# One-tile middle visits for a weight fold on two alternating PSUM banks, and one operand of the output stage made ahead of four copies

## The chip, the cores and the metric

The kernel runs on one core of a Trainium2 chip. The metric is the device time of one execution in microseconds (us), as the median of several runs. All times of single instructions come from one profiled execution of the same kernel. Engines are named as in the profile: PE is TensorE (PEld its weight loads), DVE is VectorE, ACT is ScalarE, POOL is GpSimd, and SP is SyncE, which here only issues DMAs.

## The reference, cut to what matters

Two blocks share one input `x` of 2048 tokens by 1024 features, and a gate mixes them. Block A is softmax attention with 32 heads of 32 dimensions. Block B picks, for each token and each of 32 heads, one of 64 experts by two small score tables, and adds a gated product of that expert's rows of `u` and `v`.

```
qkv = x @ wqkv                                # [2048, 3*1024], 32 heads of 32
p   = softmax(q @ k^T * 32**-0.5)             # per head
a   = (p @ v) @ wo
q1, q2 = split(x @ w_q)                       # 32 heads, 128 + 128 values each
s1, s2 = q1 @ k1^T, q2 @ k2^T                 # 8 scores each
i1, i2 = argmax(s1), argmax(s2)               # expert i1*8 + i2, one per head
b   = sum over heads of gelu(x . u[expert]) * v[expert]
g   = sigmoid(sum(x * gate_w))
out = g * a + (1 - g) * b
```

The kernel never forms `x @ w_q`. Since only the scores are wanted, it multiplies `w_q` with the differences of the rows of `k1` and `k2` first. This product of two weights is the "fold", and the change is about how it is laid into the program.

## The kernel before

Everything is float32. Most products run as three passes over a high and a low part (`split`, line 93: ACT writes the high part, DVE subtracts it). Large matrix products use a scheme with seven block products, `P1` to `P7`, in place of eight; a block product is 12 matmuls of 128x512 (`product`, lines 296 to 304, and `Halves.product`, whose matmuls are on line 964).

**Projection of q and k (0 to 377 us).** Two halves of the tokens times eight column chunks of the weight make 16 units. Units 0 and 8 are plain; `unit(u)` (line 483) makes the others, in the order P1, P5, P6, P2, P7, P3, P4, with the weight chunk of unit u+2 (`wraw`, 1 MB) loaded on SP's queue before P2. ACT and DVE prepare the next unit's operands between the products, and POOL issues the stores of q and k. Products rotate over PSUM banks 0 to 5.

**The fold inside it.** `w_q` comes as 32 tiles (`wqt`), each 1 MB in two halves of 512 KB, in four half-sized buffers, so two tiles at a time (line 313). A tile is four matmuls of 32x512 (line 341). Four tiles are a group; they accumulate in one bank, ACT copies the bank out (line 346), and later `fold_t` (line 351) transposes it in four matmuls on PE, ACT copies that (line 361), and POOL stores it. `fold()` (line 330) is a visit: it takes two tiles and then issues the loads of the next two (`load_wqs`, line 317). There is a visit after P4 of most units (`FOLDS`, line 478, and two more outside `unit`), and in the units of `MID_FOLDS` = {4, 11, 13} (line 479) a second one between P2 and P7 (line 540). All groups accumulate in bank 6, and all transposes go to bank 7. The order of each engine is the order in which the code is written, since the schedule is manual.

**Router, values, attention (377 to 1655 us).** These stages are not touched.

**Output (from 1655 us).** Eight blocks of 256 tokens are multiplied by `wo`. Blocks 0 and 1 are plain sums in banks 0 to 3 (`pa`) and 4 to 7 (`pa1`); `plain_out` (line 1582) copies the four banks to four places of one tile `post` (named `rb` in the profile), ACT and DVE in turns, and SP stores each. Both blocks use the same four places, so block 1's copies wait until block 0's stores have read them. Blocks 2 to 7 are made by `unit(n)` (line 1663) in the order P1, P7, P5, P6, P2, P3, P4, with short matmuls with `vhl` (line 1530) ahead of P2 to P4. Each product takes the next of eight banks: P1 bank 0, P7 bank 1, P5 bank 2, P6 bank 3, P2 bank 4, P3 bank 5, and so on, the same in every block. The operands `A11`, `S3`, `S1`, `S2`, `A12`, `S4`, `A22` come from the attention output (`scale_o`, line 1573, then `ht.operand`: DVE forms a sum on line 946 if the name begins with S, ACT makes the high part on line 94, DVE the low part on line 95). P7 needs S3, P5 needs S1, P6 needs S2. For block 2 only, the first four operands are made before `unit`, and S2, S4, A22 after P1's copy and after `plain_out(1, pa1)` (lines 1680 to 1683). In each block the sums that read P6, P7 and P5 out of PSUM (lines 1693 to 1696, recorded under the helper's line 970) are written behind the next block's A11, S3 and S1, so DVE does them in that order.

Of the kernel before, what the change touches and what calls it, by code (L numbers as in the profile page):

```python
# [9 lines left out]
F32 = mybir.dt.float32  # L10
F32R = mybir.dt.float32r
I32 = mybir.dt.int32
AF = mybir.ActivationFunctionType
# [6 lines left out]
KC = D // 128  # L20
HC = KC // 2
# [10 lines left out]
def gated_mha_peer_kernel(ctx, tc, xT, wqkv, wv, wo, wq, k12, ug, v, out):  # L32
# [8 lines left out]
    nc = tc.nc  # L41
# [72 lines left out]
    def bank_at(i):  # L114
        return ps1.tile([128, 512], F32, name=f"bk{i}")
# [3 lines left out]
    ev = Pool("ev", bufs=3)  # L119
    x8 = Pool("x8")  # L120
# [190 lines left out]
    def load_wq(n):  # L311
        for half in range(2):
            t = wqp.tile([128, 2, 512], F32, name="wqt", bufs=4)
            dma(t, wq[n // 4, n % 4][:, half * 1024:(half + 1) * 1024].rearrange("p (a m) -> p a m", a=2))
            wq_t[n, half] = t

    def load_wqs():
        n = fold_no[0]
        for m in range(n, min(n + 2, 32)):
            load_wq(m)  # L320

    def kpad_diffs():
        nc.gpsimd.memset(kpad, 0.0)
# [1 line left out]
            nc.gpsimd.tensor_tensor(out=kpad[:, :, i, 7 * i:7 * i + 7], in0=kraw[:, :, 1:],  # L325
                                    in1=kraw[:, :, 0:1].to_broadcast([128, 2, 7]), op=OP.subtract)

    fold_ps, fold_no, pending = [], [0], []

    def fold(load=True):  # L330

        for _ in range(2):
            n = fold_no[0]
            fold_no[0] += 1
            i = n % 4
            if i == 0:
                fold_ps[:] = [bank_at(6)]
            ps, = fold_ps
            t = wq_t.pop((n, 0)), wq_t.pop((n, 1))
            for quad in range(4):  # L340
                nc.tensor.matmul(ps[32 * quad:32 * quad + 32, :], kpad[:, quad % 2, i, :],  # L341
                                 t[quad // 2][:, quad % 2, :], start=(i == 0), stop=(i == 3))
        if i == 3:
            wt = (ev.tile([128, 512], F32, name="u4", bufs=1) if n // 4 == 3 else
                  x8.tile([128, HC, 512], F32, name="x8")[:, 0])
            nc.scalar.activation(wt, ps, AF.Copy)
            pending.append((n // 4, wt))
        if load:
            load_wqs()

    def fold_t():
        if not pending:
            return
        gi, wt = pending.pop(0)
        b, dh = divmod(gi, 2)
        pt = bank_at(7)
        for dc in range(4):
            nc.tensor.transpose(pt[:, dc * 128:(dc + 1) * 128], wt[:, dc * 128:(dc + 1) * 128], ident)
        wt2 = ev.tile([128, 512], F32, name="u7", bufs=1)[:, :448].rearrange(
            "p (a q r) -> p a q r", a=4, q=4)  # L360
        nc.scalar.activation(wt2, pt.rearrange("p (a q r) -> p a q r", a=4, q=4)[:, :, :, :28], AF.Copy)
        dma(WPD[:, 4 * dh:4 * dh + 4, 112 * b:112 * b + 112], wt2.rearrange("p a q r -> p a (q r)"),
            nc.gpsimd)
# [49 lines left out]
    for kc in range(KC):  # L413
        if kc:
            split_x(kc)
        if kc in (1, 2):
            split_w0(2 * kc, 2 * kc + 2 if kc == 1 else KC)
        if kc + 4 < KC:
            load_x(0, kc + 4)
        if kc == 3:  # L420
            load_w(1)
        if kc == 4:
            for n in range(2):
                load_wq(n)
        if kc == HC:
            gate_mm(range(HC))
        if kc == KC - 2:
            gate_mm(range(HC, KC))
        order = [(n, i) for i in range(3) for n in range(2)]
        if kc in (0, KC - 1):  # L430
            order = [(n, i) for n in range(2) for i in range(3)]
        for w in range(2):
            for n, i in order:
                plain_mm(w, n, kc, i, kc == 0 and i == 0, kc == KC - 1 and i == 2)
# [41 lines left out]
    load_w(2)  # L476
    fold()
    FOLDS = {1, 2, 3, 4, 5, 6, 8, 9, 10, 11, 12, 13}
    MID_FOLDS = {4, 11, 13}

    NUNIT = 2 * KC

    def unit(u):
        p, c, v = u // KC, CHUNK[u], u + 1
        n0 = TOK0[p] // 512
        seven = v < NUNIT and v != KC
        turns = (dict(P2=("S1+", "S3+", "A11"), P7=("S1", "S2+", "S2"), P3=("S4+", "A12"), P4=("S3", "S4"))
                 if u % KC == 1 else
                 dict(P1=("S1+", "S3+", "A11"), P5=("S1", "S2+"), P6=("S2", "S4+"), P2=("A12",),
                      P7=("S3",), P3=("S4",), P4=("A22",)))  # L490
# [36 lines left out]
        hook("P6")  # L527
        add(u2, c1, p6)
        add(u4, u2, p5)
        ready("P6")  # L530
        if v + 1 < NUNIT and v + 1 != KC:
            load_w(v + 1)
        p2 = product("P2")
        if u % KC == 2:
            fold_t()
        hook("P2-")
        add(c1, c1, p2)
        evac(0, c, n0, c1, p2, True)
        if u in MID_FOLDS:
            fold()  # L540
        hook("P2")
        ready("P2")
        p7 = product("P7")
        hook("P7-")
        u7 = place("u7")
        add(u7, u4, p7)
        add(u2, u2, p7)
        evac(1, c, n0 + 1, u7, p7, True)
        hook("P7")
        ready("P7")  # L550
        p3 = product("P3")
        hook("P3-")
        add(u4, u4, p3)
        evac(0, c, n0 + 1, u4, p3, True)
        hook("P3")
        ready("P3")
        p4 = product("P4")
        add(u2, u2, p4)
        evac(1, c, n0, u2, p4, True)
        if u in FOLDS:  # L560
            fold(u != KC - 2)
        hook("P4")
        ready("P4")

# [26 lines left out]
    for u in range(1, KC):  # L591
        unit(u)
# [967 lines left out]
    ht = Halves(lambda name: wk.tile([128, 512], F32, name="ssb"), bank)  # L1560
# [102 lines left out]
    def unit(n):  # L1663
# [14 lines left out]
        c1 = osb()  # L1678
        nc.scalar.activation(c1, p1, AF.Copy)
        if n == 2:  # L1680
            plain_out(1, pa1)
            for name in ("S2", "S4", "A22"):
                ht.operand(name)
        if n + 2 < S // W:
            load_chunk(n + 2, 0, KC)
# [85 lines left out]
```

## Time and profile before

| What | Value |
|---|---|
| Median of 3 runs (lowest, highest) | 1840.55 us (1836.91, 1843.77) |
| The profiled execution's own time | 1842.35 us |
| Its span, first to last instruction | 1840.5 us |
| Projection, 0 to 376.8 us | PE busy 368.86 us, 254 GB/s of DMA |
| Router, 376.8 to 465 us | PE busy 87.90 us, 119 GB/s |
| Values and experts, 465 to 628 us | PE busy 162.45 us, 193 GB/s |
| Attention, 628 to 1655 us | PE busy 1026.08 us, 170 GB/s |
| Output, 1655 to 1840.5 us | PE busy 178.01 us, 176 GB/s |

A row of the timeline reads: start in us from the span's beginning, duration, engine, line, operation, what is written and read, shapes, and how many instructions the row merges; a bracket at the end holds the idle time ahead of it and what ended that. On PE each product appears as rows of up to 12 matmuls. A matmul's recorded end overlaps the next one's start, so times on PE are best taken from start to start. The granted clock is 1.00 at full speed.

### The profile page before, as it was taken

Reading aid. Unit: us, or ns where it says so; the run is one execution under the profiler, and the core shown is the slowest. Engines: PE = TensorE matmul, PEld = TensorE weight load, DVE = VectorE, ACT = ScalarE, POOL = GpSimd, SP = SyncE. Lnnn points to the kernel's source line nnn. Section 1 sums busy time; section 2 is a strip of 40 time slices with the busy share of each in tenths; the row PEclk is TensorE's granted clock in tenths of the full one; section 3 lists DMA queues with packets and bytes.
Section 4 is the critical chain, followed back from the end, with each engine's and each line's share of the span. In section 5 each row is a group of like instructions: output and inputs, shape, how many; then the busy total and the mean of one; then the engine's idle time right before and its main releaser. Section 6 shows DMA issues by size and latency. Waiting matters only on the chain.

```text
span 1840.5 us, 26554 instructions
## 1 busy us (share of the span) xinstructions
PE 1823.3 (99%) x10083; PEld 1102.1 (60%) x10083; DVE 1461.7 (79%) x1258; ACT 1312.7 (71%) x1716; POOL 231.3 (13%) x358
## 2 busy tenths in 40 slices
PE   9999999999999999999999999999999999999999
PEld 6767777788888644444444444444444444447787
DVE  7856975689976888888888888988888888885674
ACT  5544644531342599999999999999999999993221
POOL 1222222244101200000000000000000000000000
PEclk9999999999999999999999999999999999999999
DMA  7897688760257767777777777777776777766872
GB/s 270 275 289 227 235 274 262 233 225 17 81 185 250 242 154 180 163 161 166 167 187 163 181 172 169 178 165 183 168 182 162 171 164 174 186 136 189 280 161 76
DMA packets 127441, 345.24 MB, mean 188 GB/s; under 512 B 17168, under 2 KB 57904, under 8 KB 107920
## 3 DMA queue, kind: packets, MB, share of 16 engines
q1 hardware_dynamic: 95688, 193.40, 35.6%
q0 software_dynamic: 28224, 145.92, 34.2%
q10 hardware_dynamic: 3400, 4.20, 0.8%
q8 instruction: 80, 1.31, 0.3%
q14 instruction: 49, 0.40, 0.1%
HBM read 171.76 MB, written 72.36 MB: 133 GB/s over the span
## 4 chain that ended last, share of the span: by engine, by line
PE 88%; DMA 6%; issue 3%; DVE 1%; ACT 1%; POOL 1%; SPq 1%; ACTq 0%; DVEq 0%; POOLq 0%
PE ring L1318 28%; PE o L1339 25%; PE bk L302 14%; PE pa L964 6%; PE bk L725 5%; PE bk L983 2%; PE bk L290 2%; DMA wqt<-in_wq 2%; PE bk L341 2%; PE ring L1352 1%; PE bk L964 1%; DMA accd<-rd 1%; PE pa L1530 1%; DMA out<-rb 1%; DMA accd<-P 1%
## 5 line engine op out<-in xcount | busy, mean ns | idle before, releaser
L1328 ACT ACTIVATE P<-ring 128x1024 f32<-128x1024 f32 (+2 forms) x1031 | 912.5, 983 | 14.6 <-DMA accd<-P 2.5
L1368 DVE TENSOR_TENSOR acc<-acc,P 128x2048 f32<-128x2048 f32 x319 | 730.9, 2291 | 72.6 <-ACT P L1328 47.1
L1339 PE MATMUL o<-P,V 128*32 128x512 f32 x3840 | 464.8, 599 | 0.0
L1318 PE MATMUL ring<-Q,K 98*128 98x512 f32 x1024 | 272.2, 407 | 0.3 <-ACT P L1328 0.2
L1318 PE MATMUL ring<-z,z 98*128 98x512 f32 x1020 | 270.6, 407 | 0.6 <-ACT accd L1328 0.6
L1318 PEld LDWEIGHTS ring<-Q,K 98*128 98x128 f32 x1024 | 182.0, 188 | 144.8 <-ACT P L1328 72.8
L1318 PEld LDWEIGHTS ring<-z,z 98*128 98x128 f32 x1020 | 181.3, 188 | 142.8 <-ACT P L1328 72.0
L1339 PEld LDWEIGHTS o<-P,V 128*32 128x32 f32 x3840 | 98.8, 109 | 223.0 <-issue 214.3
L1361 POOL DMA_DIRECT2D accd<-P x95 | 81.5, 858 | 931.4 <-ACT P L1328 367.8
L1366 DVE TENSOR_TENSOR acc<-P,P 128x2048 f32<-128x2048 f32 x32 | 73.4, 2293 | 74.6 <-ACT P L1328 74.6
L302 PE MATMUL bk<-xh,A 128*128 128x512 f32 x336 | 85.7, 406 | 0.0
L302 PE MATMUL bk<-xh,S 128*128 128x512 f32 x336 | 81.2, 392 | 0.0
L302 PE MATMUL bk<-xl,S 128*128 128x512 f32 x336 | 80.1, 390 | 0.0
L302 PEld LDWEIGHTS bk<-xh,A 128*128 128x128 f32 x336 | 64.2, 194 | 24.7 <-issue 5.9
L135 ACT ACTIVATE hi<-u 128x512 fp32r<-128x512 f32 x42 | 26.6, 632 | 70.2 <-issue 38.2
L1371 DVE TENSOR_TENSOR acc<-acc,accd 128x2048 f32<-128x2048 f32 x32 | 73.1, 2285 | 0.0
L302 PEld LDWEIGHTS bk<-xl,S 128*128 128x128 f32 x336 | 62.8, 188 | 14.8 <-issue 0.8
L302 PEld LDWEIGHTS bk<-xh,S 128*128 128x128 f32 x336 | 62.5, 188 | 13.8 <-issue 0.8
L1328 ACT ACTIVATE accd<-ring 128x1024 f32<-128x1024 f32 (+2 forms) x64 | 62.2, 1032 | 2.3 <-PE ring L1318 2.2
L964 PE MATMUL pa<-woh,acc 128*128 128x512 f32 x192 | 62.2, 389 | 0.0
L512 DVE TENSOR_TENSOR u<-u,bk 128x512 f32<-128x512 f32 x70 | 46.6, 682 | 10.0 <-PE bk L302 5.4
L138 DVE TENSOR_TENSOR A<-wraw,A 128x512 fp32r<-128x512 f32 x42 | 28.9, 688 | 28.0 <-ACT A L135 27.9
(302 smaller groups left out, 2193.3 us busy)
## 6 DMA issues: line engine op xcount, KB each, us to landing
accd<-P POOLq DMA_DIRECT2D x95, 1024.0 KB, 7.7
wqt<-in_wq SPq DMA_DIRECT2D x64, 512.0 KB
wraw<-in_wqkv SPq DMA_DIRECT2D x28, 512.0 KB
kdh<-hi POOLq DMA_DIRECT2D x32, 256.0 KB, 6.3
kdl<-lo POOLq DMA_DIRECT2D x32, 256.0 KB, 7.2
qdh<-hi POOLq DMA_DIRECT2D x32, 256.0 KB, 6.4
qdl<-lo POOLq DMA_DIRECT2D x32, 256.0 KB, 6.5
z<-kdh SPq DMA_DIRECT2D x32, 256.0 KB
```

The costliest lines, as they stand in the source:

```text
L290: nc.tensor.matmul(b0[w, n], AW[PLAIN[w, ki]][a][:, k, :], X[f"B{ki + 1}{n + 1}"][b][:, k, :], start=first, stop=last)
L302: nc.tensor.matmul(ps, a[i][:, k, :], b[j][:, k, :], start=(k == 0 and i == j == 0), stop=(k == HC - 1 and i == 1))
L512: nc.vector.tensor_tensor(out=out, in0=a, in1=b, op=OP.add)
L725: nc.tensor.matmul(ps, x_part(a, t // 4, kc)[:, tok], b, start=first, stop=last)
L964: nc.tensor.matmul(ps, self.a[a][i][:, k, :], self.b[b][j][k], start=(not first and k == 0 and i == j == 0), stop=(k == HC - 1 and i == 1))
L1318: on_ring(nc.tensor.matmul(ring[:, i, :], K[:98, kt * 128:(kt + 1) * 128], Q[:98, qc * 512:(qc + 1) * 512], start=True, stop=True), i)
L1328: on_ring(nc.scalar.activation(P[h, kt][:, q0 * 512:(q0 + m) * 512].rearrange("p (a m) -> p a m", a=m), ring[:, i:i + m, :], AF.Exp, scale ...
L1339: nc.tensor.matmul(O[h][32 * qc:32 * qc + 32, :], Vt[g][:, kt, 32 * j:32 * j + 32], p[:, qc * 512:(qc + 1) * 512], start=(kt == 0), stop=( ...
L1361: nc.gpsimd.dma_start(ACCD[h], P[h, kt], accum_op=OP.add)
L1366: nc.vector.tensor_add(ACC[h], P[h, 0], P[h, kt])
L1368: nc.vector.tensor_add(ACC[h], ACC[h], P[h, kt])
L1371: nc.vector.tensor_add(ACC[h], ACC[h], ACCD[h])
```

## The change

It has two parts that do not touch each other. In the fold, a visit may take one tile: `fold(tiles=1)`. The three middle visits of two tiles, in units 4, 11 and 13, become six of one tile, in units 3, 5, 10, 11, 12 and 13. The visits after P4 keep two tiles. Loading is now counted by tiles loaded (`wq_no`), so a visit of one tile issues one tile's two loads. Since a group can now end in the middle of a visit, ACT's copy moves inside the loop, and groups alternate between banks 6 and 7; a group's transposes go to the bank in which it accumulated. In the output stage, block 2's operand S2 is made ahead of `plain_out(1, pa1)`; S4 and A22 stay behind it.

```
-        n = fold_no[0]
-        for m in range(n, min(n + 2, 32)):
-            load_wq(m)
+        while wq_no[0] < min(fold_no[0] + 2, 32):
+            load_wq(wq_no[0])
+            wq_no[0] += 1
...
-    def fold(load=True):
-
-        for _ in range(2):
+    def fold(tiles=2, load=True):
+
+        for _ in range(tiles):
             n = fold_no[0]
             fold_no[0] += 1
-            i = n % 4
+            gi, i = divmod(n, 4)
             if i == 0:
-                fold_ps[:] = [bank_at(6)]
+                fold_ps[:] = [bank_at(6 + gi % 2)]
...
-        if i == 3:
...
+            if i == 3:
+                wt = (ev.tile([128, 512], F32, name="u4", bufs=1) if gi == 3 else
+                      x8.tile([128, HC, 512], F32, name="x8")[:, 0])
+                nc.scalar.activation(wt, ps, AF.Copy)
+                pending.append((gi, wt))
...
-        pt = bank_at(7)
+        pt = bank_at(6 + gi % 2)
...
-    MID_FOLDS = {4, 11, 13}
+    MID_FOLDS = {3, 5, 10, 11, 12, 13}
...
         if u in MID_FOLDS:
-            fold()
+            fold(1)
...
         if n == 2:
+            ht.operand("S2")
             plain_out(1, pa1)
-            for name in ("S2", "S4", "A22"):
+            for name in ("S4", "A22"):
                 ht.operand(name)
```

The first place is PE in units 3 and 4. A `bk` row on line 302 is one product of 12 matmuls, an L341 row is fold matmuls (four to a tile), and the numbers tell tiles of the same name apart. Before, from P2 of unit 4 to P1 of unit 5:

```order
L302 MATMUL bk_1103<-xl_151,A_933 128x512 x12
L341 MATMUL bk_1120<-wqt,kpad 32x512 x8
L302 MATMUL bk_1141<-xh_427,S_959 128x512 x12
L302 MATMUL bk_1167<-xl_152,S_983 128x512 x12
L302 MATMUL bk_1191<-xh_441,A_1025 128x512 x12
L341 MATMUL bk_1120<-wqt,kpad 32x512 x8
L302 MATMUL bk_1233<-xh_149,A_1051 128x512 x12
```

The changed kernel has no middle visit in unit 4; from P2 of unit 3 to P1 of unit 4 it has this:

```order
L302 MATMUL bk_916<-xl_151,A_755 128x512 x12
L341 MATMUL bk_829<-wqt,kpad 32x512 x4
L302 MATMUL bk_945<-xh_427,S_781 128x512 x12
L302 MATMUL bk_971<-xl_152,S_805 128x512 x12
L302 MATMUL bk_995<-xh_441,A_846 128x512 x12
L341 MATMUL bk_829<-wqt,kpad 32x512 x4
L341 MATMUL bk_1021<-wqt,kpad 32x512 x4
L302 MATMUL bk_1038<-xh_149,A_872 128x512 x12
```

Eight fold matmuls between P2 and P7 became four, and the visit after P4 closes one group (`bk_829`) and opens the next in another bank (`bk_1021`). PE's number of matmuls is unchanged.

The second place is DVE in the output stage, around block 2's copies. `s_12798` holds S3 and S1, `acc` A11, A12, S4 and A22, `z_12825` S2, and `rb_5505` is `post`. Before, from the low part of A12 on:

```order
L95 TENSOR_TENSOR acc<-V,acc 128x512
L1587 COPY rb_5505<-pa_12671 128x512
L1587 COPY rb_5505<-pa_12673 128x512
L946 TENSOR_TENSOR V<-ssb,V 128x4x128
L95 TENSOR_TENSOR z_12825<-V,z_12825 128x512
L946 TENSOR_TENSOR V<-V 128x4x128
```

In the changed kernel, whose lines here are lower by one:

```order
L95 TENSOR_TENSOR acc<-V,acc 128x512
L945 TENSOR_TENSOR V<-ssb,V 128x4x128
L95 TENSOR_TENSOR z_12825<-V,z_12825 128x512
L1586 COPY rb_5505<-pa_12671 128x512
L1586 COPY rb_5505<-pa_12673 128x512
L945 TENSOR_TENSOR V<-V 128x4x128
```

S2's sum and low part moved ahead of the two copies; on ACT, S2's high part moved ahead of its two copies in the same way. SP's order in the output stage is unchanged.

More of the change, by code (lines that the diff above doesn't have):

```diff
@@ L326, in kpad_diffs @@
                                     in1=kraw[:, :, 0:1].to_broadcast([128, 2, 7]), op=OP.subtract)
-    fold_ps, fold_no, pending = [], [0], []
-    def fold(load=True):
-        for _ in range(2):
+    fold_ps, fold_no, wq_no, pending = [], [0], [0], []
+    def fold(tiles=2, load=True):
+        for _ in range(tiles):
             n = fold_no[0]
             fold_no[0] += 1
-            i = n % 4
+            gi, i = divmod(n, 4)
             if i == 0:
-                fold_ps[:] = [bank_at(6)]
+                fold_ps[:] = [bank_at(6 + gi % 2)]
             ps, = fold_ps
@@ L342, in fold @@
                                  t[quad // 2][:, quad % 2, :], start=(i == 0), stop=(i == 3))
-        if i == 3:
[L344 to L347, printed above, removed]
+            if i == 3:
[3 more added lines that the diff above has]
+                pending.append((gi, wt))
         if load:
@@ L422, in gated_mha_peer_kernel @@
         if kc == 4:
-            for n in range(2):
-                load_wq(n)
+            load_wqs()
         if kc == HC:
@@ L560, in unit @@
         if u in FOLDS:
-            fold(u != KC - 2)
+            fold(load=u != KC - 2)
         hook("P4")
```

## The prediction

> **What bounds the kernel now.** The first view is the page's table of engines, the second the list of who waited for whom, for PE.
>
> ```profile
> PE 1823.3 (99%) x10083; PEld 1102.1 (60%) x10083; DVE 1461.7 (79%) x1258; ACT 1312.7 (71%) x1716; POOL 231.3 (13%) x358
> ```
>
> ```profile
> PE bk L341 <- DMA wqt<-in_wq: 5.6, 3, 2.6
> PE pa L964 <- ACT z L94: 3.2, 1, 3.2
> ```
>
> PE is busy for 99% of the span, so time is won only where PE waits or runs slowly. The list names two places of any size: the fold waits three times for its tiles, 5.6 us in all, and one output product waits once for ACT. The change works at exactly these two. What each costs in full is read from PE's timeline, since a wait can be followed by a slow stretch. First the fold: a visit that waits for nothing (the middle one of unit 4), with two products behind it.
>
> ```profile
> 112.22 1.92 PE L341 MATMUL bk<-wqt,kpad 128*32 128x512 f32 x16
> 114.07 3.06 PE L302 MATMUL bk<-xh,S 128*128 128x512 f32 x12
> 116.97 2.88 PE L302 MATMUL bk<-xl,S 128*128 128x512 f32 x12
> ```
>
> Then the visits that end units 4, 11 and 13, one after the other.
>
> ```profile
> 122.50 1.95 PE L341 MATMUL bk<-wqt,kpad 128*32 128x512 f32 x12
> 127.04 1.05 PE L341 MATMUL bk<-wqt,kpad 128*32 128x512 f32 x4 [2.59 <-DMA wqt<-in_wq]
> 128.03 4.61 PE L302 MATMUL bk<-xh,A 128*128 128x512 f32 x12
> 132.47 2.90 PE L302 MATMUL bk<-xl,S 128*128 128x512 f32 x12
> ```
>
> ```profile
> 283.84 2.10 PE L341 MATMUL bk<-wqt,kpad 128*32 128x512 f32 x12
> 287.92 1.24 PE L341 MATMUL bk<-wqt,kpad 128*32 128x512 f32 x4 [1.99 <-DMA wqt<-in_wq]
> 289.09 4.40 PE L302 MATMUL bk<-xh,A 128*128 128x512 f32 x12
> 293.33 2.89 PE L302 MATMUL bk<-xh,S 128*128 128x512 f32 x12
> ```
>
> ```profile
> 334.00 2.02 PE L341 MATMUL bk<-wqt,kpad 128*32 128x512 f32 x12
> 337.04 1.05 PE L341 MATMUL bk<-wqt,kpad 128*32 128x512 f32 x4 [1.01 <-DMA wqt<-in_wq]
> 338.02 3.06 PE L302 MATMUL bk<-xh,A 128*128 128x512 f32 x12
> 340.91 2.89 PE L302 MATMUL bk<-xh,S 128*128 128x512 f32 x12
> ```
>
> The undisturbed visit with the product behind it takes 116.97 - 112.22 = 4.75 us. The three that wait take 132.47 - 122.50 = 9.97, 293.33 - 283.84 = 9.49 and 340.91 - 334.00 = 6.91 us. They lose 5.22, 4.74 and 2.16 us, **12.1 us** together, twice the listed wait. Part of the rest is a slow product: behind the waits of 2.59 and 1.99 us it takes 4.44 and 4.24 us where 114.07 to 116.97 gives 2.90; behind 1.01 us it takes 2.89. The granted clock explains it: 0.57 in the four us behind the first wait. The columns are the stretch and its length, PE, PEld, DVE, ACT and POOL busy with counts, granted clock, DMA share and GB/s; the other two rows are units 3 and 11, for later.
>
> ```profile
> 128.00:132.00 4.00, 4.00 (x12) 3.13 (x11) 1.90 (x3) 1.11 (x2) 0.00 (x0) 0.57 1.01 317
> 77.60:98.70 21.10, 21.10 (x101) 16.07 (x100) 16.39 (x26) 11.21 (x25) 5.41 (x10) 1.00 0.85 287
> 260.60:289.10 28.50, 26.51 (x134) 16.85 (x133) 19.94 (x31) 13.68 (x30) 7.06 (x14) 0.99 0.99 293
> ```
>
> **The fold, part by part.** In each waiting row group, 12 of 16 instructions (six of eight matmuls with their weight loads) ran without the long wait; only the last half tile was missing. SP shows why:
>
> ```profile
> 113.31 15.15 SPq L76 DMA_DIRECT2D wqt<-in_wq  x8
> ```
>
> A middle visit of two tiles frees all four half buffers at once, from 113.31 on, and all four halves (2 MB) are wanted again three products later, at 122.50. Three halves arrived for their turn, the fourth only at 127.04. With one tile per middle visit, two halves are asked for there. The visit after P4 then begins with a tile that was requested one visit earlier, and wants the new one a tile later, at about 122.50 + 1.85/2 = 123.4 on this scale (1.85 is 114.07 - 112.22). In the trace, three halves were there by then. So two are, with a half to spare, if the engines of the DMA are no more loaded than here: all 12.1 us go.
>
> They could be more loaded. A unit with a middle visit now moves 3 MB of `wqt`, 1 MB of `wraw` and 2 MB of stores: 6.29 million bytes. Unit 3 above, without one, took 21.1 us; a tile more (0.93) makes 22.0: 286 GB/s, four units in a row (10 to 13). Unit 3 itself moved 287 at a DMA share of 0.85 and nothing waited; unit 11 moved 293 at 0.99 and PE waited. The need is nearest to unit 3, so I take **no wait**. The bounds: at best nothing; at worst each of the six pairs is as late as the old ones.
>
> What is added: the same 128 fold matmuls, but 19 visits instead of 16. A product behind a visit takes 2.90 us; undisturbed it takes 2.72 (68 matmuls of this shape run from 1739.98 to 1755.40 in the rows of the output below, so 12 take 12 x 15.42 / 68). Three visits more cost 3 x 0.18 = **0.5 us**. The alternating banks cost nothing by the order: a bank is reused two groups later, and its transposes are copied out a unit or more before. One buffer is held longer: group 2 now ends in the middle of unit 5, so its copy, which lies in `x8`, is transposed in unit 6, and the load into `x8` must follow it.
>
> ```profile
> 153.35 1.25 SPq L76 DMA_DIRECT2D x<-in_xT  x1
> ```
>
> The load now starts at 153.35, early in unit 6, and would come after that unit's P5. SP has only unit 8's small weight load behind it there, and the data are wanted in P6 of unit 7. The cover is a whole unit, 21 us, so the cost is nothing; without it, the first split of unit 7 would wait by as much as the load is late. Fold in all: 12.1 - 0.5 = **11.6 us**. PE idles for 1840.5 - 1823.3 = 17.2 us in all, and 8.8 of these are the two listed waits, so everything behind is bound by PE too and should come earlier by 11.6.
>
> **The output part.** On PE, DVE and ACT, in this order:
>
> ```profile
> 1710.96 2.88 PE L964 MATMUL pa<-wo_raw,s 128*128 128x512 f32 x12
> 1717.09 4.54 PE L964 MATMUL pa<-wo_raw,z 128*128 128x512 f32 x12 [3.24 <-ACT z L94]
> 1734.54 0.39 PE L964 MATMUL pa<-z,s 128*128 128x512 f32 x1
> 1739.98 2.88 PE L964 MATMUL pa<-wo_raw,z 128*128 128x512 f32 x12
> 1755.40 0.39 PE L964 MATMUL pa<-z,s 128*128 128x512 f32 x1
> ```
>
> ```profile
> 1708.02 0.68 DVE L95 TENSOR_TENSOR acc<-V,acc 128x512 fp32r<-128x512 f32 x1
> 1713.41 0.69 DVE L1587 COPY rb<-pa 128x512 f32<-128x512 f32 x1 [4.70 <-DMA out<-rb]
> ...
> 1715.69 0.68 DVE L946 TENSOR_TENSOR V<-ssb,V 128x512 f32<-128x512 f32 x1
> ...
> 1721.92 1.22 DVE L1577 TENSOR_TENSOR V<-V,accd 128x1024 f32<-128x1024 f32 x1 [1.57 <-DMA V<-od]
> ...
> 1729.33 0.68 DVE L970 TENSOR_TENSOR rb<-osb,pa 128x512 f32<-128x512 f32 x1
> 1730.05 2.01 DVE L970 TENSOR_TENSOR rb<-rb,pa 128x512 f32<-128x512 f32 x3
> ...
> 1751.03 2.01 DVE L970 TENSOR_TENSOR rb<-rb,pa 128x512 f32<-128x512 f32 x3
> ```
>
> ```profile
> 1716.41 0.63 ACT L94 ACTIVATE z<-V 128x512 fp32r<-128x512 f32 x1 [0.56 <-DVE V L946]
> ```
>
> P5 of block 2 starts at 1710.96, so PE could begin P6 at 1713.68. It begins at 1717.09, 0.05 us after S2's high part ends, and its recorded 4.54 us are 1.66 more than a product's 2.88, a slow clock again. S2's sum stood behind DVE's copies, which waited 4.70 us for block 0's stores. Moved ahead, it starts when DVE is free, at 1708.70, and is done with sum 0.68, high part 0.63 and low part 0.68 by about 1710.8: 2.9 us before P6. In block 3, P6 to the next block's P7 takes 1755.40 - 1739.98 = 15.42 us; so P7 of block 3 could start at 1713.68 + 15.42 = 1729.10 instead of 1734.54. That is 5.4 us.
>
> But something else is late next. P7 of block 3 writes bank 1, which holds P7 of block 2 until DVE's first sum of the row at 1730.05 has read it, at 1730.72. That sum stands behind block 3's A11, S3 and S1, which begin when `V<-od` lands (1721.92), and S2's move does not hasten that load. PE would wait 1.6 us there and start P7 at 1730.75: the gain is 1734.54 - 1730.75 = 3.8 us. In block 4 the same bank is free at 1751.03 + 0.67 = 1751.70, and P7 would want it at 1755.40 - 3.8 = 1751.6: 0.1 us more. Output: **3.7 us**. The copies, which now come behind S2, still wait for the stores and end as now; P2's bank, the first copy's, is free at 1713.41 + 0.69 = 1714.1, before P2 wants it at 1713.68 + 2.72 = 1716.4.
>
> The wait of 1.6 us has one unknown: whether the clock drops behind it. The rows bound it: after 1.01 us it did not, after 1.99 us it did, for 4.24 - 2.90 = 1.3 to 4.44 - 2.90 = 1.5 us. It is nearer to the second. But the slow stretch behind the first wait was (1 - 0.57) x 4 / 0.5 = 3.4 us long at half speed, and if the clock is judged by stretches of that length, a boundary splits a wait of 1.6 us about half of the time (1.6 / 3.4) into parts like the harmless one. So I take nothing, and give the drop a large chance of its own, with 1.5 us in the range.
>
> [...]
>
> **The sum.** 1842.35 - 11.6 - 3.7 = 1827.05 us for an execution like the profiled one, which lies 1.8 us above the median of the runs; the same subtraction from the median gives 1825.25. I forecast **1826 us**.
>
> **The rivals.**
> - *The clock drops behind the new bank wait.* Price 1.5 us: 1827.5. For it and against it: the two bounds and the split, as above. Chance 0.25.
> - *S2 was not what P6 waited for last*: its other operand, loaded into `wo_raw`, may have landed little earlier, or the move does not take effect. Then the output gives nothing, 1829.7. Against it: P6 started 0.05 us after ACT, and that load was issued ahead of the stores whose landing released the copy at 1713.41. Chance 0.06.
> - *Tiles still late in the row of units 10 to 13.* If these lose what units 11 and 13 lose now, 4.74 + 2.16 = 6.9 us stay: 1832.9. For it: the share of 0.99 in unit 11. Chance 0.12.
> - *Slower: all six pairs starve.* The pair must land within about 10 us of the middle visit's first request (113.31 to 123.4). If the stores of q and k, on the same DMA engines, push it beyond that in all six units, each loses the present mean of 4.0 us: 24.2 instead of 12.1, so 1826 + 24.2 = 1850.2 us, slower than before. Against it: three halves land in that time today. Chance 0.07.
>
> **How the numbers follow.** The forecast has 0.50, with its own range of 1822 to 1829. About 0.5%, or 9.2 us, is what a measurement of this kernel can tell from no change, so "faster" ends at 1831.3. Forecast and the first two rivals lie below: 0.81. The third is "same": 0.12. The fourth is "slower": 0.07. A range of 1821.5 to 1834 holds the first four cases with their unknowns and leaves out the last and a few oddities.
>
> **What would show it.** Right: PE's waits hold no `wqt` row, or under 1 us; the granted clock is 1.00 from 100 to 350 us; the projection ends near 365 us; six rows of one-tile visits of about 0.95 us. In the output, P6 of block 2 follows P5 without a gap, and a new wait of PE for DVE's sum stands ahead of P7 of block 3, about 1.6 us. Wrong: `wqt` waits in units 10 to 13, or the output's gap moved whole to the bank or to `wo_raw`.

## The result and the profile after

| | Before | Changed |
|---|---|---|
| Median of the runs measured together | 1841.49 us (6 runs, 1836.91 to 1844.99) | 1831.47 us (6 runs, 1829.67 to 1832.57) |
| Ratio, 95% interval | | 0.9946 (0.9930 to 0.9963) |
| The profiled execution's own time | 1842.35 us | 1832.25 us |
| Its span | 1840.5 us | 1830.4 us |
| PE reaches the router at | 376.77 us | 365.27 us |
| From attention's last matmul to PE's last | 181.31 us | 182.51 us |

The kernel became 10.0 us faster, 0.54%; the interval reaches from 6.8 to 12.9 us. The forecast was 1826 us, the time is 1831.47. The last two rows, from the two profiled executions, tell where it differs: the projection gave 11.50 us (forecast 11.6), but the output, forecast to give 3.7, became 1.2 us longer. The stages between moved by 0.2 us.

The table of engines of the changed kernel, and its list of PE's waits:

```profile
PE 1817.8 (99%) x10083; PEld 1099.8 (60%) x10083; DVE 1461.4 (80%) x1258; ACT 1312.5 (72%) x1716; POOL 231.7 (13%) x358
```

```profile
PE pa L963 <- DVE rb L969: 2.3, 1, 2.3
...
PE pa L1522 <- ACT z L94: 1.4, 1, 1.4
PE pa L963 <- ACT osb L1678: 0.8, 1, 0.8
```

Both rows of before are gone: no wait for `wqt`, none for S2's high part. Three others stand in the output: 2.3 us for DVE's sums, 1.4 and 0.8 us ahead of that.

First the fold. PE's timeline of unit 3 shows its new middle visit, of one tile, between P2 and P7, and the visit after P4. The next two rows are the pair of unit 13, the last of the four units in a row. The window below them is the whole projection, with the columns named in the prediction.

```profile
90.26 1.07 PE L341 MATMUL bk<-wqt,kpad 128*32 128x512 f32 x8
91.25 3.02 PE L302 MATMUL bk<-xh,S 128*128 128x512 f32 x12
94.11 2.88 PE L302 MATMUL bk<-xl,S 128*128 128x512 f32 x12
96.83 2.88 PE L302 MATMUL bk<-xh,A 128*128 128x512 f32 x12
99.64 1.92 PE L341 MATMUL bk<-wqt,kpad 128*32 128x512 f32 x16
101.50 3.06 PE L302 MATMUL bk<-xh,A 128*128 128x512 f32 x12
...
315.28 1.06 PE L341 MATMUL bk<-wqt,kpad 128*32 128x512 f32 x8
...
324.66 1.92 PE L341 MATMUL bk<-wqt,kpad 128*32 128x512 f32 x16
```

```profile
0.00:365.30 365.30, 363.30 (x1807) 272.21 (x1808) 266.43 (x363) 189.26 (x362) 81.20 (x153) 1.00 0.80 262
```

Start follows start without a gap (90.26, 91.25, 94.11, 96.83, 99.64), and the granted clock is 1.00 for the whole projection. All six one-tile rows are 1.06 or 1.07 us long, and the visits after them 1.92, like the undisturbed one of the prediction. (An L341 row counts matmul records, of which the trace has 256 for the program's 128 matmuls. So x8 is one tile. The prediction took its "12 of 16 instructions" for matmuls and weight loads together; they are matmuls alone, two records each. That the last half tile was missing is right all the same.) Now PE in the output: P5 and P6 of block 2, P7 to P6 of block 3, P7 of block 4, and PE's last product.

```profile
1702.18 2.88 PE L963 MATMUL pa<-wo_raw,s 128*128 128x512 f32 x12
1704.90 2.88 PE L963 MATMUL pa<-wo_raw,z 128*128 128x512 f32 x12
...
1722.73 0.67 PE L963 MATMUL pa<-z,s 128*128 128x512 f32 x1 [2.26 <-DVE rb L969]
...
1727.15 2.90 PE L963 MATMUL pa<-wo_raw,s 128*128 128x512 f32 x12
1729.89 2.88 PE L963 MATMUL pa<-wo_raw,z 128*128 128x512 f32 x12
...
1745.30 0.39 PE L963 MATMUL pa<-z,s 128*128 128x512 f32 x1
```

P6 of block 2 follows P5 by 2.72 us, the undisturbed time: S2's wait is gone. P7 of block 3 waits 2.26 us for bank 1 and then takes 4.42 us to P5, 1.7 more than P5 takes to P6; the granted clock was 0.50 from 1722.83 to 1726.24. DVE shows what held the bank:

```profile
1699.58 0.69 DVE L945 TENSOR_TENSOR V<-ssb,V 128x512 f32<-128x512 f32 x1
1701.02 0.69 DVE L95 TENSOR_TENSOR z<-V,z 128x512 fp32r<-128x512 f32 x1 [0.76 <-ACT z L94]
...
1713.45 1.23 DVE L1576 TENSOR_TENSOR V<-V,accd 128x1024 f32<-128x1024 f32 x1 [3.99 <-DMA V<-od]
...
1721.18 0.68 DVE L969 TENSOR_TENSOR rb<-osb,pa 128x512 f32<-128x512 f32 x1
1721.90 2.01 DVE L969 TENSOR_TENSOR rb<-rb,pa 128x512 f32<-128x512 f32 x3
```

S2 is ready 3.2 us ahead of P6 (1701.02 + 0.69 against 1704.90). DVE then waits 3.99 us for block 3's V, where it waited 1.57 before. Its sums free the bank at 1721.90 + 0.67 = 1722.57, and P7 starts 0.16 later.

V is the last link of a chain of small DMAs that begins at attention's end: the row sums go out (`smd`), come back rearranged (`rr`), go out and come back (`rd`, `accd`), and SP's queue goes on behind them. Of the chain of work that ended last, these are two links before, and the same two after:

```profile
1661.49 8.54 DMA smd<-ssb
...
1684.94 11.93 DMA accd<-rd
```

```profile
1650.21 10.26 DMA smd<-ssb
...
1675.14 12.44 DMA accd<-rd
```

The same store of the same bytes landed 1.72 us later after its issue. The change touches nothing there. So the first question is whether this belongs to the change or to the execution.

### The profile page after: what moved, and what is told of

Same layout as the page of the kernel before. It is cut to its first block, busy times and chain, and to the rows that moved or that the text cites. A ratio compares the mean times of both kernels' runs of the same rounds, so it can differ in the third digit from the quotient of the medians.

```text
span 1830.4 us, 26559 instructions
## 1 busy us (share of the span) xinstructions
PE 1817.8 (99%) x10083; PEld 1099.8 (60%) x10083; DVE 1461.4 (80%) x1258; ACT 1312.5 (72%) x1716; POOL 231.7 (13%) x358
## 4 chain that ended last, share of the span: by engine, by line
PE 88%; DMA 5%; issue 3%; DVE 1%; ACT 1%; SPq 1%; POOL 1%; DVEq 0%; ACTq 0%; POOLq 0%
PE ring L1317 28%; PE o L1338 25%; PE bk L302 15%; PE pa L963 5%; PE bk L724 5%; PE bk L982 2%; PE bk L290 2%; PE bk L341 2%; PE ring L1351 1%; PE bk L963 1%; SPq L76 1%; DMA accd<-rd 1%; DMA accd<-P 1%; DMA smd<-ssb 1%; DMA z<-t2h 1%
## 5 line engine op out<-in xcount | busy, mean ns | idle before, releaser
L94 ACT ACTIVATE acc<-V 128x512 fp32r<-128x512 f32 x24 | 14.5, 625 | 50.8 <-DVE V L1576 14.4
```

## The experiments

All profiles are compared in one table, in us after the start of attention's last matmul (the last row `o<-P,V`) except for the second column. "Landed" is when SP issues the DMA that follows the `smd` store; P6(2) is the start of P6 of block 2, and so on. Undisturbed, P6(2) to P7(3) is 15.42 and P7(3) to P7(4) 20.86.

| Profile | Router at | Landed | Scaling of block 3 | P6(2) | P7(3) | P6(3) | P7(4) | Last matmul |
|---|---|---|---|---|---|---|---|---|
| before | 376.77 | 15.55 | 67.37 | 62.54 | 79.99 | 85.43 | 100.85 | 181.31 |
| before, again (e8) | 373.62 | 15.28 | 66.23 | 61.15 | 78.59 | 84.03 | 99.44 | 179.91 |
| two tiles, two banks (e3) | 373.89 | 15.95 | 68.70 | 62.49 | 79.94 | 85.38 | 100.80 | 181.26 |
| fold alone (e1) | 365.75 | 15.31 | 66.07 | 61.19 | 78.44 | 83.88 | 99.29 | 179.76 |
| S2 alone (e2) | 376.84 | 14.21 | 66.74 | 58.92 | 75.89 | 81.43 | 96.85 | 177.31 |
| S2 alone, again (e11) | 371.01 | 17.73 | 69.92 | 61.07 | 79.18 | 86.34 | 101.75 | 182.22 |
| changed | 365.27 | 17.28 | 70.19 | 61.64 | 79.47 | 86.63 | 102.04 | 182.51 |
| changed, again (e6) | 366.65 | 16.29 | 67.30 | 59.36 | 76.03 | 81.55 | 97.84 | 178.42 |
| changed, a third (e12) | 366.22 | 16.20 | 69.11 | 60.28 | 77.84 | 83.38 | 98.79 | 179.26 |
| bank 1 copied out (e4) | 366.37 | 17.65 | 68.67 | 61.00 | 76.41 | 81.89 | 99.24 | 179.84 |
| V first (e5) | 365.35 | 15.52 | 64.12 | 59.39 | 75.57 | 81.01 | 98.73 | 180.95 |
| V first, bank copied (e7) | 367.15 | 18.27 | 65.31 | 61.41 | 76.82 | 82.26 | 100.22 | 182.42 |
| V on GpSimd's queue (e9) | 366.39 | 15.72 | 66.74 | 65.33 | 80.75 | 86.19 | 101.60 | 182.07 |
| V of blocks 3 and 4 there (e10) | 366.30 | 16.52 | 66.55 | 60.18 | 76.30 | 81.74 | 97.16 | 177.62 |

**Each part alone.** The changed kernel with the old output part (e1), and the kernel before with the new one (e2):

```
 e1:     if n == 2:
-            ht.operand("S2")
             plain_out(1, pa1)
-            for name in ("S4", "A22"):
+            for name in ("S2", "S4", "A22"):
 e2: the reverse edit, in the kernel before
```

> The fold part alone, with the output stage as before. Theory A (the fold gave all of its 11.5 us, and the output part gave nothing because a later wait took its place): 11 to 12 us faster than the kernel before, so about 1830, the projection's end near 365.3 us as in the changed kernel, and the wait of 3.2 us ahead of P6 of block 2 still there. Theory B (the fold gave less in the mean than in the profiled execution, and the output part gave its 3.7 us): 6 to 7 us faster, about 1835.

Measured: 1832.1 us (7 runs, 1829.7 to 1834.71), ratio 0.9951 (0.9934 to 0.9968), and no `wqt` row among the waits. PE's timeline has P6 of block 2 waiting as before, with a slow product behind it:

```profile
1704.66 4.72 PE L963 MATMUL pa<-wo_raw,z 128*128 128x512 f32 x12 [2.10 <-ACT z L94]
```

The fold gives about 9 us of the 10 (interval 5.9 to 12.2), and in the projection of this profile 376.77 - 365.75 = 11.0. The time lies between those of the two theories and excludes neither; that S2's wait is still there, 2.10 us instead of 3.2, is what theory A said.

> The output part alone, with the fold as before. Theory A: the wait ahead of P6 of block 2 goes and a wait for DVE's sums ahead of P7 of block 3 comes, with or without a clock drop: between 1.5 us slower and 3.8 us faster than before, less than 2 us either way in the median. Theory B: 3.7 us faster. Theory C (making S2 earlier holds up the copies, the stores or the loads behind them): over 1.5 us slower, with the copies of block 1 or the load of block 3's operand later after the end of attention than in the kernel before.

Measured: 1838.49 us (12 runs, 1830.93 to 1844.8), ratio 0.9981 (0.9963 to 0.9998): 3.5 us, with an interval from 0.4 to 6.8. The waits of PE:

```profile
PE bk L341 <- DMA wqt<-in_wq: 5.9, 5, 2.9
...
PE pa L964 <- DVE rb L970: 1.4, 1, 1.4
```

S2's wait is gone and the new one for bank 1 is here too, without any change in the fold: the wait belongs to the S2 edit, as theory A had it. The time does not choose: its interval holds theory B's 3.7 us and also less than 2. In this profile the landing was early (14.21), the wait 1.4 us, P7 behind it took 2.82 us to P5 (1731.16 to 1733.98), and the output was 4.0 us shorter than before's. The same kernel a second time (e11):

> The kernel before with only the output part of the change, for a second profile. Theory (the fold's stalls differ between executions, and the output part gains about 2 us): the projection ends between 373.5 and 377 us with waits for tiles; P6 of block 2 has no wait, P7 of block 3 waits 0.5 to 2.3 us for bank 1; the last product starts 177 to 180 us after attention's last. Rival (3.7 us in every execution): 177.5 us or less.

Measured: 1837.87 us for the one execution; landing at 17.73, and this wait on PE:

```profile
1728.35 0.47 PE L964 MATMUL pa<-z,s 128*128 128x512 f32 x1 [2.53 <-DVE rb L970]
```

The granted clock was 0.50 behind it (1729.10 to 1732.51), and the output was 0.9 us longer than before's. Two expectations failed: the projection ended at 371.01 us, earlier than 373.5, and the last product started later than 180. One kernel, 177.31 and 182.22 us: what happens behind attention differs between executions by more than the edit was forecast to give.

**The banks without the smaller visits (e3).** The fold's new counting and alternating banks, but two tiles in the middle visits of the old units, and the old output:

```
-    MID_FOLDS = {3, 5, 10, 11, 12, 13}
+    MID_FOLDS = {4, 11, 13}
-            fold(1)
+            fold()
```

> The fold with three middle visits of two tiles as before, but groups in banks 6 and 7 in turns, loads counted by tiles and the copy inside the loop; output as before. If the size of the middle visits is what counts: same as before within 1.5 us, with three waits for the tiles of 1 to 2.6 us. If the alternating banks gave part of the gain: 2 us faster or more, with shorter waits.

Measured: 1842.78 us (12 runs, 1838.93 to 1846.46), ratio 1.0007 (0.9993 to 1.0020). The waits:

```profile
PE bk L341 <- DMA wqt<-in_wq: 4.1, 3, 2.3
PE pa L963 <- ACT z L94: 2.7, 1, 2.7
```

The banks alone do nothing, and three waits for tiles are back. The gain of the fold comes from the six one-tile visits in place of the three of two tiles; their size and their new places were not taken apart.

**The bank freed by another engine (e4).** ACT copies block 2's P7 out of bank 1 to SBUF, and DVE's sum reads the copy:

```
-        ahead("A11")
+        if n > 2:
+            ahead("A11")
         p7 = ht.product("P7")
+        if n == 2:
+            t7 = fin.tile([128, 512], F32, name="t7")
+            nc.scalar.activation(t7, p7, AF.Copy)
+            p7 = t7
+            ahead("A11")
```

> The changed kernel, but ACT copies P7 of block 2 out of its bank as soon as it is done, and DVE's sum reads the copy; one ACT instruction more, nothing else moved but block 3's A11, which stands behind that copy. Theory A: PE's wait of 2.3 us ahead of P7 of block 3 goes, about 0.8 us appears ahead of P5 (its bank is freed by the same sums, 2.0 us later), the clock stays at 1.00 there, and the time is 3 us below the changed kernel's, about 1828.5. Theories B and C: no change from the changed kernel, about 1831.5, as PE would wait for something else at the same point.

Measured: 1831.04 us (6 runs, 1829.04 to 1833.02), ratio 0.9942 (0.9924 to 0.9961), level with the changed kernel's, not 3 us below it as theory A expected. P7 of block 3 follows P6 of block 2 by 15.41 us although the landing was late (17.65): bank 1 was what P7 waited for. The wait of 0.8 us expected ahead of P5 did not come (1721.08 to 1723.80, 2.72 us). But the next turn of the bank waits:

```profile
1743.91 0.47 PE L963 MATMUL pa<-z,s 128*128 128x512 f32 x1 [1.78 <-DVE rb L969]
```

That is P7 of block 4: DVE's sums of block 3 are late now. The wait moved on by one block.

**The load that DVE waits for, earlier (e5), and both (e7).** In e5 block 3's V and row sums are issued ahead of `woh` and `wol`; e7 adds the copy of e4.

```
-    load_t(3, *([part[k][:, 512:] for k in range(HC)] for part in (woh, wol)))
     load_rb(3, 0, KC, queue=nc.scalar)
     load_o(3, 0, KC)
+    load_t(3, *([part[k][:, 512:] for k in range(HC)] for part in (woh, wol)))
```

> The changed kernel, with the loads of block 3's V and of its row sums written ahead of the loads of the last matrix operands (woh, wol), so SP and ACT issue them earlier. Theory (bank 1 is held because block 3's scaling stands ahead of DVE's sums and waits for V, whose load is the last link of a chain of DMAs from the end of attention): block 3's scaling begins several us earlier than 70.2 us after the last attention product, DVE's sums of block 2 earlier than 77.9, P7 of block 3 follows 15.4 us behind P6 of block 2 with no wait, the clock does not drop there, and the output stage is 2 to 4 us shorter than in the changed kernel: about 1828 us. Rival (DVE's sums are late from DVE's own work, not from V): scaling and sums do not move, the wait of about 2 us stays, same time as the changed kernel, 1831.5. Second rival (what is pushed back now arrives too late): PE waits for woh or wol at P4 or P6 of block 2, same time or longer.

Measured: 1830.08 us (6 runs, 1828.33 to 1832.86), ratio 0.9925 (0.9904 to 0.9946). DVE, block 3's scaling, the sums of block 2, block 4's scaling; then PE:

```profile
1708.28 2.35 DVE L1576 TENSOR_TENSOR V<-V,accd 128x1024 f32<-128x1024 f32 x2
...
1717.42 0.69 DVE L969 TENSOR_TENSOR rb<-osb,pa 128x512 f32<-128x512 f32 x1 [2.03 <-DMA out<-rb]
...
1734.31 2.36 DVE L1576 TENSOR_TENSOR V<-V,accd 128x1024 f32<-128x1024 f32 x2 [6.13 <-DMA accd<-rd]
```

```profile
1714.31 0.50 PE L963 MATMUL pa<-wol,acc 128*128 128x512 f32 x1 [0.40 <-DMA wol<-t3l]
1742.89 0.47 PE L963 MATMUL pa<-z,s 128*128 128x512 f32 x1 [2.15 <-DVE rb L969]
```

DVE no longer waits for V, and PE not for bank 1 in block 3. Three other things are late next, as a staircase: the sums now wait 2.03 us for block 1's stores (they write the tile that these read), `wol` is 0.40 us late at P4, and block 4's row sums, behind all this on SP, make DVE wait 6.13 us and PE 2.15 in block 4, and from there the last matmul is 82.22 us away where e10 has 80.46. The first rival is out, since the scaling moved from 70.19 to 64.12; the second was partly right, by the 0.40 us. The output, 180.95, is where before's two profiles are (181.31, 179.91), and the 2 to 4 us expected did not come: e5's median is 1.6 us below that of the changed kernel measured beside it (e6, 1831.66), within the spread of the runs.

> Both at once in the changed kernel: V of block 3 loaded ahead of the last matrix operands, and ACT copies block 2's P7 out of bank 1, so that the bank no longer waits for DVE. Theory: no wait for a bank in blocks 3 and 4; P7 of block 3 15.4 us behind P6 of block 2; output 3 to 4 us shorter than in the changed kernel, 1827 to 1829 us. Rival (the wait only moves to a later block, since DVE's sums stay behind the same load): P7 of block 4 waits about 1.9 us, about 1830.

Measured: 1830.6 us (6 runs, 1827.61 to 1833.94), ratio 0.9925 (0.9903 to 0.9946). Its rival came: P7 of block 4 waits 2.39 us (row below). Here the landing was the latest of all, 18.27, and PE also waited 2.19 us for block 1's operands.

```profile
1671.83 1.20 PE L1522 MATMUL pa<-woh,z 128*128 128x512 f32 x4 [2.19 <-ACT z L94]
1745.23 0.47 PE L963 MATMUL pa<-z,s 128*128 128x512 f32 x1 [2.39 <-DVE rb L969]
```

**The changed kernel twice more (e6, e12), and the kernel before once more (e8).** No edit.

> The changed kernel itself, once more. Theory (the first leg of the DMA chain, the landing of the small store of the row sums, differs between executions and sets how long PE waits for bank 1): the landing lies anywhere between 14 and 18 us after the last attention product, the sums of block 2 follow 58 to 61 us behind it, and the wait at P7 of block 3 is that time less the product's own, 0.5 to 3 us; the projection ends at 365.3 us again within 0.6. Rival (the change itself makes the chain longer): landing at 17 us or later again, wait of 2.3 us again.

Measured: 1831.66 us (6 runs, 1828.99 to 1834.95), ratio 0.9936 (0.9914 to 0.9958). The projection ended at 366.65 us, a little outside the 0.6 us. The landing was at 16.29 and the first wait 1.10 us, so the rival, 17 or later and 2.3 us again, did not come. Two waits for the bank, and a mean granted clock of 1.000 (0.999 in the changed profile):

```profile
1720.47 0.47 PE L963 MATMUL pa<-z,s 128*128 128x512 f32 x1 [1.10 <-DVE rb L969]
1742.28 0.47 PE L963 MATMUL pa<-z,s 128*128 128x512 f32 x1 [0.71 <-DVE rb L969]
```

> The changed kernel, for a third profile. Theory: the projection ends at 365.3 to 367.2 us with no wait for tiles; PE waits 0.5 to 2.5 us for bank 1 in block 3 or 4; the clock halves only if PE idles for more than about half of one stretch of 3.41 us; the last product starts 178 to 182.5 us after attention's last.

Measured: 1829.46 us for the one execution, landing at 16.20, and a wait of 1.98 us in block 3, again with a mean granted clock of 1.000:

```profile
1721.57 0.47 PE L963 MATMUL pa<-z,s 128*128 128x512 f32 x1 [1.98 <-DVE rb L969]
```

> The kernel before, once more, for a second profile. Theory: three waits for tiles in the projection of together 2 to 6 us, with the projection's end between 373.5 and 377 us; P6 of block 2 waits for S2's high part by about 3 us; the small store of the row sums lands between 14 and 18 us after the last attention product. Rival (the landing is fixed by the program's order): 15.5 us within 0.3 again.

Measured: 1837.7 us for the one execution. PE's waits:

```profile
PE bk L341 <- DMA wqt<-in_wq: 4.9, 5, 2.8
PE pa L964 <- ACT z L94: 2.1, 1, 2.1
```

The waits for tiles are there, five now instead of three, yet the projection ended 3.15 us earlier than in the profile that the prediction used: the granted clock was 1.00 behind the longest of them, where it was 0.50 behind two there, and the mean over the execution was 0.999 against 0.997. The landing was at 15.28, within 0.3 of 15.5 as the rival expected; what the ten profiles with the S2 edit say to that is told under "What stays open".

**V on GpSimd's queue (e9), and block 4's loads too (e10).**

```
-    load_o(3, 0, KC)
+    load_o(3, 0, KC, nc.gpsimd)
 e10 also:
-            load_chunk(n + 2, 0, KC)
+            load_chunk(n + 2, 0, KC, nc.gpsimd if n == 2 else nc.sync)
```

> The changed kernel, with block 3's V loaded on GpSimd's queue instead of SP's, so that these loads wait only for their own buffers, and the loads of woh and wol keep their place on SP. Theory (the sums that hold bank 1 stand behind this load): block 3's scaling no longer waits for V, as in the run with V ahead on SP; woh and wol are issued at 52 us after the last attention product, not 62, and PE does not wait for them; P7 of block 3 follows P6 of block 2 by 15.4 us, or waits under 1 us for block 1's stores, which DVE's sums must not overwrite. About 1829 us. Rival (V lands late because the DMA engines are busy, whoever issues it): scaling still waits 3 to 4 us and P7 of block 3 1 to 2.3 us, 1831.5.

Measured: 1833.09 us (6 runs, 1831.23 to 1836.09), ratio 0.9962 (0.9947 to 0.9977), not faster than the changed kernel. Scaling begins at 66.74 and the wait for bank 1 is gone, but one that neither theory had stands ahead of P7 of block 2. Two rows of the chain of work, and PE's:

```profile
1675.79 15.66 DMA accd<-rd
...
1692.85 9.29 DMA z<-t2h
```

```profile
1702.27 0.76 PE L963 MATMUL pa<-z,s 128*128 128x512 f32 x1 [3.00 <-DMA z<-t2h]
```

The load of the row sums took 15.66 us where the profiles above had 11.93 and 12.44, what stands behind it on SP was later (`woh` was issued at 56.8, not at 52), and the granted clock was 0.50 from 1701.64 to 1708.47. Whether V, now moving at the same time, made it 15.66 was not shown; e10, with V moving there too, has 14.25.

> The same, with block 4's V and row sums on GpSimd's queue too, so that they do not stand behind block 1's stores on SP. Theory: DVE's scaling of block 4 comes earlier than 87 us after the last attention product, its sums of block 3 free bank 1 ahead of P7 of block 4, no wait of PE for a bank in blocks 3 and 4, and the last product starts 177 to 178 us after attention's last: 1827.5 to 1829 us. Rival (the buffers of V and of the row sums are free too late for an earlier load): the same as the run with block 3's V alone.

Measured: 1829.51 us (6 runs, 1826.83 to 1829.9), ratio 0.9940 (0.9927 to 0.9953), just above the 1827.5 to 1829 expected. The three largest waits of PE:

```profile
PE bk L408 <- DVE ident L90: 1.4, 1, 1.4
PE pa L1522 <- ACT z L94: 0.9, 1, 0.9
PE bk L290 <- ACT xh L94: 0.8, 1, 0.8
```

No wait for a bank in blocks 3 and 4 and a mean granted clock of 1.000; the last matmul starts at 177.62, as the theory had it. Yet block 4's scaling began at 87.09, not earlier than 87, so DVE gained little. Its ratio lies among those of the changed kernel (0.9946, 0.9936): that it is the better one is possible and not shown.

## Why the prediction was right in one half and not in the other

**The fold: the mechanism right.** No `wqt` wait stands in any of the nine profiles with one-tile visits, the six pairs did not starve, units 10 to 13 ran dry nowhere, and the projection of the changed profile ended at 365.27 us where 376.8 - 11.6 makes 365.2. e3 shows that the visits did it and not the banks.

**But its size was one draw.** The 12.1 us were added up in one execution. The five profiles with two-tile visits reach the router at 371.01 to 376.84, on average 374.43 us; the nine others at 365.27 to 367.15, on average 366.16. The typical gain is 8.3 us, and the profile that the prediction read was within 0.1 us of the slowest of the five. The step "all 12.1 us go" was right; that 12.1 us are the usual loss was never tested. That the two profiled executions give 11.50 where 11.6 was forecast is therefore luck: the one is among the slowest of its five, the other the fastest of its nine.

**S2: the cause right, the gain not.** S2 was what P6 waited for: with it ahead, P6 follows P5 with no gap. What was then late was foreseen as well, DVE's sums behind block 3's scaling, holding bank 1 (e2, e11, e6, e12 show it, e4 takes it away). The step that failed is the one that put a date on it, "start P7 at 1730.75", with V landing when it landed in the profile of before, and P6 as soon as PE was through with P5. Both hang on the chain of DMAs from attention's end. For the changed profile, with attention's last matmul as zero (1654.55 before, 1643.26 after):

| | Forecast | Measured | Later by |
|---|---|---|---|
| P6 of block 2 | 1713.68 - 1654.55 = 59.13 | 61.64 | 2.5 |
| P7 of block 3, less 15.42 from P6 | 76.20 - 74.55 = 1.6 | 79.47 - 77.06 = 2.4 | 0.8 |
| P7 of block 3 to P5 | 2.72 | 4.42 | 1.7 |
| P7 of block 4, its own wait | 0.1 | 0 | -0.1 |
| PE's last matmul | 181.31 - 3.7 = 177.6 | 182.51 | 4.9 |

The first row is the chain: the list of waits has 1.4 us on line 1522 for operands of block 1 and 0.8 us ahead of P7 of block 2, both in code that was not touched. (The list names ACT's copy for the second; the chain of work names the landing of `z<-t2h`, P7's matrix operand, issued behind V's chain on SP.) They are 2.2 of the 2.5 us. Over all profiles the first of these waits goes with the landing: six of the seven with a landing at 16.20 or later have it, with 0.9 to 2.2 us (e6 has none), and of the seven at 15.95 or earlier none waits there for more than 0.4. The second is the same chain through V. The third is the first rival, the clock behind the bank wait: it came (a granted clock of 0.50), at 1.7 us instead of 1.5.

**What the S2 edit is worth.** The five profiles that have it without further edits end at 177.31, 178.42, 179.26, 182.22 and 182.51 us, on average 179.9; the four without it at 179.76 to 181.31, on average 180.6. Counted from the landing instead, they average 163.6 and 165.0. That is 0.6 to 1.4 us instead of 3.7, from few profiles with a spread of 5 us; e2's timing alone (0.4 to 6.8 us) admits more. The edit removes a wait with its slow product, but it lets PE run up to the next limit, and that limit moves with the landing: the two late landings among the five (17.28 and 17.73) are the two that end last. They are also the only two of the five in which the granted clock fell to 0.50 behind the bank wait, 1.7 us of their lateness. With the fold in place, the timings give the S2 edit 1.0 us (10.0 less e1's 9.0) or, by e6's ratio, 2.8 (11.8 less 9.0), both within the noise.

**The sum.** 8.3 and 0.6 to 1.4 us make 8.9 to 9.7, beside a measured 10.0. The forecast took off 15.3: the fold's usual gain was 3.3 us less than its term of 11.6, the output's 2.3 to 3.1 less than its 3.7. That 1831.47 still lies in the range of 1821.5 to 1834 is luck as well: its upper part was there for late tiles in units 10 to 13, which did not come, and the forecast's own range ended at 1829.

**What stays open.** Why the `smd` store takes 7.3 us (landed at 14.21 less its issue at 6.95) in one execution and 11.3 (18.27) in another was not found; no run isolated it. In the packed trace the store is four packets of 2048 bytes that move for 0.08 us each; before, they start at 13.49, 13.74, 14.57 and 14.89, in the changed profile at 13.23, 13.24, 14.83 and 16.41. So the last packets start late rather than move slowly.

Nor is it excluded that the S2 edit has a part in it. The four profiles without it land at 15.28 to 15.95, on average 15.5; the ten with it at 14.21 to 18.27, on average 16.5. Against it: SP's order is the same, and on DVE and ACT the first instruction that stands elsewhere runs 53 us after attention's last matmul, long after the landing; and the same kernel landed at 14.21 (e2) and 17.73 (e11). Four profiles against ten are too few to settle it. If the edit has no part in the landing, 1.4 us is the fairer price for it, else 0.6.

## What to carry to other kernels

When a prediction adds up stalls that come from late DMAs, take them from more than one execution: here the same projection lost between 5 and 11 us to its tiles (371.01 and 376.84 less 366.16). When a wait goes, follow what stands behind it past the first successor: here bank, V, block 1's stores and block 4's row sums made an engine wait in turn (2.26, 3.99, 2.03 and 6.13 us), and taking away one gave the next. And when a load moves ahead on a queue, price what is issued behind it too: in e5 `wol` came 0.40 us late, and DVE waited 6.13 us for block 4's row sums.

## What the runs showed of the hardware

This is what the profiles show of the granted clock. Before, three half-clock stretches begin at 128.23, 288.66 and 1718.84 us, 47 and 419 steps of 3.413 us apart, and each lasts one step; the one at the program's end lasts 4.30 us, and in e9 two steps follow each other (1701.64 to 1708.47). With the exceptions below, half clock followed where PE idled long enough within one step of this grid, whatever the length of the wait. The columns are those named in the prediction. Before, the wait of 2.59 us at 127.04 and the stretch behind it:

```profile
124.82:128.23 3.41, 1.19 (x5) 0.35 (x6) 0.69 (x1) 0.73 (x4) 1.08 (x2) 1.00 1.04 135
128.23:131.64 3.41, 3.41 (x9) 2.64 (x9) 1.90 (x3) 1.03 (x2) 0.00 (x0) 0.50 1.00 317
```

The kernel before, again (e8): PE idles longer at the same place, but a boundary of the grid cuts the idle time in two.

```profile
123.24:126.65 3.41, 2.04 (x12) 0.22 (x12) 1.98 (x3) 1.49 (x4) 1.19 (x3) 1.00 1.14 273
126.65:130.07 3.42, 1.83 (x8) 0.86 (x9) 0.00 (x0) 0.73 (x2) 0.43 (x1) 1.00 0.96 169
130.07:133.48 3.41, 3.41 (x17) 2.81 (x16) 1.90 (x3) 1.53 (x5) 0.00 (x0) 1.00 1.02 383
```

Behind 2.22 us of idleness in one stretch (3.41 - 1.19) the clock was 0.50; behind 1.37 and 1.59 us in two, 2.96 together, it was 1.00. The exception is the wait of 3.24 us ahead of P6 of block 2, before, which a boundary cut into almost equal parts:

```profile
1712.02:1715.43 3.41, 1.82 (x9) 1.17 (x7) 1.04 (x2) 0.78 (x2) 0.00 (x0) 1.00 1.05 402
1715.43:1718.84 3.41, 1.75 (x6) 1.16 (x7) 2.24 (x4) 1.49 (x3) 0.00 (x0) 1.00 1.03 367
```

Idle 1.59 and 1.66 us, and the stretch behind the second was at half clock (0.50). Up to PE's last product, seven stretches with 1.99 us of idleness or more stand in the windows of these profiles (1.99 and 2.22 before, 2.03 in e8, 2.07 in e7, 2.26 in the changed profile, 2.37 in e9, 2.53 in e11), and half clock followed each. Of the four from 1.66 to 1.85 (before, 1.68 in e11, 1.78 in e4, 1.85 in e7) only the first was followed by it, and none of 1.59 (before and e8) and 1.37 (e8); but behind e9's first half stretch, with 0.63 us of idleness, the clock stayed at 0.50. So in these profiles the outcome changed between 1.59 and 1.99 us, about half of a stretch. The four between are not in the order of their idleness (half clock followed 1.66 and not 1.85), and what decides there stays open.

A wait of 1.99 us cost 1.3 us before, at 287.92 (a product of 4.24 us instead of 2.90), and the 2.26 us of the changed profile 1.7 (4.42 instead of 2.72). Behind 1.98 us in e12 the product took 2.82; how that wait lay across the stretches is not shown. The prediction's guess, that stretches are judged and a boundary can split a wait, fits e8's wait and not the exception.
